# Fourier mixing and soft mixture of experts on one core: mirror rows folded in place, weights placed in freed tiles, one text order for all queues

## The chip, the cores and the metric

The kernel runs on one core of one Trainium2 chip. The metric is device time in microseconds of one execution, inputs and output in HBM. Engines are named as in the profile: PE is TensorE, DVE is VectorE, ACT is ScalarE, POOL is GpSimd, SP is the sync engine, whose queue issues all DMAs here.

## The reference

All tensors are float32. The first part is the real part of a two-dimensional Fourier transform of each of 8 sequences; the second routes all 19,968 tokens softly through 32 slots of 8 experts.

```python
X = np.fft.fft(x, axis=1)                     # x: 8 x 2496 x 256
x = np.fft.fft(X, axis=2).real.reshape(19968, 256)
logits = x @ phi                              # phi: 256 x 32
d = softmax over the tokens of logits         # per slot
slot_input = (d.T @ x).reshape(8, 4, 256)
for e in range(8):
    h = np.maximum(slot_input[e] @ w1[e], 0)  # w1: 8 x 256 x 1024
    slot_out[e] = h @ w2[e]                   # w2: 8 x 1024 x 256
c = softmax over the slots of logits          # per token
return c @ slot_out
```

## The kernel before

The 8 sequences are worked on as 4 pairs (`NPAIR`). The transform is never written out: logits come from x and a transformed phi, and the slot inputs come from x weighted by back-transformed softmax weights. As the output of a real transform has mirrored parts, each row of x is first added to its mirror row (the fold). A pair has four x tiles (t = 0 to 3) of 128 x 2560: plain rows in the first half of the columns, mirror rows in the second.

The parts, each a function named by its letter, for pair p:

- `load_x` (L174): one DMA of 1,280 KB per tile into one of 5 "ring" buffers. All 16 are issued in order.
- a (L230): the fold into a new tile eo (12 buffers), on DVE for the first tile and on POOL for the other 15 (L233); DVE transposes it into xT (L235; 4 buffers).
- z (L237): PE multiplies xT by the transformed phi (wz) into four PSUM banks; z of half h needs two xT tiles.
- t (L252): four DVE transposes bring the banks into zt (L257), after a memset on POOL (L254).
- b (L259): PE does the first transform stage (tile `a`, L266), ACT evicts.
- c (L269): for each half `hf`, PE does the second stage (lp, lm; L278, L279); ACT and DVE form the logits lt (L280 to L283); DVE takes maxima mx (L286); PE transposes them (mt, L288); DVE reduces and spreads them (L290, L292); PE transposes back (L293); DVE copies the result nm (L295); ACT takes exp into d (L298); POOL forms sum and difference dpm (L300, L301).
- e, d (L304, L322): PE transforms dpm back; ACT evicts to esb and dsb.
- u (L340): PE multiplies the weights by the folded rows eo (L354) into a bank, and ACT keeps the sum of the pair.

Then m (L389) joins the four pairs to slot inputs, l (L433) and v (L447) are the two layers of the experts in two halves, r (L459) gives rh. For the token softmax, s (L473) transposes lt, x, y, g (L490 to L508) do maximum, exp and division, q (L510) transposes the result to ct, and o (L518) multiplies ct by rh, evicts alternately by ACT and DVE into ring buffers and writes the output, 20 tiles.

The weights (w1 8.4 MB, w2 8.4 MB) are loaded by `load_w` (L373) in 22 DMAs after all x loads: five ring buffers, twelve eo buffers, four xT buffers and one more ring buffer take them (`WTILES`, L128), so each waits until the tile that it replaces has been used.

Order: `ORDER` (L29) lists the parts with their pair and half. `in_order` (L550) chains the instructions of each named engine in this order; up to r that is PE alone (`CHAIN = ("PE",)`), from r on PE, DVE, ACT and POOL. DVE, ACT, POOL and SP are ordered by the scheduler's own estimate before that. In `ORDER`, c of a half holds everything from lp to dpm, so that on PE the maxima's two transposes of half 0 come before lp of half 1.

Of the kernel before, what the change touches and what calls it, by code (L numbers as in the profile page):

```python
# [134 lines left out]
def _build(nc, tc, xh, phih, w1h, w2h, cins, where, out):  # L135
# [4 lines left out]
    with ctx:  # L140
# [197 lines left out]
        anchor = {}  # L338

        def part_u(p):  # L340
            ps = bank3(f"tok{p}")
            for h in range(2):
                for g in range(4):
                    pe.matmul(
                        ps[32 * g : 32 * g + 32, 0:1], dsb[p][:, 0, h, 0, 0, :], C("onehot"),
                        start=h == 0, stop=h == 1, tile_position=(0, 32 * g),
                    )
            sc.copy(tok[:, p : p + 1], ps[:, 0:1])
            ub = pu.tile([128, 512], F32, name=f"u{p}", tag="u")
            rows = [(h, ah, q) for h in range(2) for ah in range(2) for q in range(NQ)]  # L350
            for cc in range(10):
# [10 lines left out]
            ubs.append(ub)
            if p == NPAIR - 1:
                anchor["u"] = last.ins

        for p in range(NPAIR):
            for t in range(4):
                if (p, t) not in xt:
                    load_x(p, t)
# [3 lines left out]
        def load_w():  # L373
            cs.append(cp.tile(list(cins[4].shape), F32, name="cs4"))
            nc.sync.dma_start(cs[4], cins[4])
            for k, (first, kind, n) in enumerate(WTILES):
                t = {"ring": ring, "eo": eu, "et": et}[kind](f"w{k}")
                src, of, bw = (w1h, w1t, 512) if first else (w2h, w2t, D)
# [260 lines left out]
```

## Time and profile before

| | |
|---|---|
| median of 3 runs | 251.22 us (249.47, 252.27, 251.22) |
| the profiled execution | 249.02 us, its span 247.2 us |
| busy: PE, DVE, ACT, POOL | 68%, 44%, 31%, 32% |
| DMA | 59.83 MB, mean 242 GB/s over the span |
| chain that ended last, by engine | PE 41%, DVE 26%, DMA 14%, issue 5%, ACT 4%, POOL 4% |
| mean granted clock of PE | 0.861 |

The span runs from the first to the last instruction of the execution. The chain is the work that ended last, followed back from the end: at each step to what released it. "Issue" is time in which an engine waited for nothing that the profile shows. PE does each float32 matmul as two recorded instructions, so xcounts on PE are twice the number of matmuls in the program (transposes are single).

### The profile page before, as it was taken

To read this page: it belongs to the slowest core of one execution; us is meant where nothing else is said; L and a number is where in the kernel's file an instruction comes from. 1 tells how busy PE (TensorE), PEld (TensorE's weight loads), DVE (VectorE), ACT (ScalarE), POOL (GpSimd) and SP (SyncE) were. 2 spreads that over 40 slices of the span, in tenths; PEclk is the share of its full clock that TensorE was granted. 3 is DMA by queue.
4 is the path that set the end of the run, shared out by engine and by line. 5 is a ranking of instruction groups with operands and counts; after the bars stand their busy time and mean duration, and the time that the engine had idled before them with its cause. 6 is when DMAs were issued, how large, how long until landed. Compare 5 with 4: busy or idle time off the path is not lost.

```text
span 247.2 us, 5345 instructions
## 1 busy us (share of the span) xinstructions
PE 168.4 (68%) x2320; PEld 106.7 (43%) x2320; DVE 108.4 (44%) x183; ACT 75.7 (31%) x176; POOL 78.5 (32%) x55
## 2 busy tenths in 40 slices
PE   0576309559755986648879549959994989878800
PEld 0465208258522564514566125644462354344500
DVE  0543271444844046441004440040776689996410
ACT  2000003322324222332025331401541578653400
POOL 0288699841003892032000032000354144440000
PEclk9999999659985799965999957997999799997555
DMA  6999999994000099200846007592200399999995
GB/s 217 424 425 420 425 426 434 427 431 193 3 0 0 3 347 422 90 0 33 295 186 215 0 3 223 204 320 107 86 3 0 127 414 429 423 423 422 424 429 227
DMA packets 9672, 59.83 MB, mean 242 GB/s; under 512 B 1200, under 2 KB 1584, under 8 KB 5040
## 3 DMA queue, kind: packets, MB, share of 16 engines
q1 hardware_dynamic: 9648, 59.48, 60.0%
q8 instruction: 18, 0.29, 0.5%
q14 instruction: 6, 0.05, 0.1%
HBM read 39.03 MB, written 20.45 MB: 241 GB/s over the span
## 4 chain that ended last, share of the span: by engine, by line
PE 41%; DVE 26%; DMA 14%; issue 5%; ACT 4%; POOL 4%; SPq 1%; DVEq 0%; ACTq 0%
DMA x<-xh 10%; PE u L354 10%; PE z L245 7%; DVE o L536 5%; PE a L266 5%; DMA out<-o 4%; DVE zt L257 4%; PE e L313 4%; PE h L438 3%; DVE mx L286 3%; PE po L531 2%; POOL eo L233 2%; ACT d L298 2%; DVE cm L505 2%; PE lp L278 2%
## 5 line engine op out<-in xcount | busy, mean ns | idle before, releaser
L233 POOL TENSOR_TENSOR eo<-x 128x1280 f32<-128x1280 f32 x15 | 43.3, 2894 | 15.4 <-DMA x<-xh 15.0
L531 PE MATMUL po<-ct,rh 32*128 32x512 f32 (+2 forms) x192 | 35.2, 630 | 5.3 <-DVE o L536 1.9
L235 DVE STREAM_TRANSPOSE xT<-eo 128x1280 f32<-128x1280 f32 x16 | 23.9, 1502 | 32.5 <-PE z L245 18.4
L245 PE MATMUL z<-xT,wz 32*64 32x160 f32 x1024 | 27.5, 358 | 7.3 <-issue 3.8
L245 PEld LDWEIGHTS z<-xT,wz 32*64 32x64 f32 x1024 | 23.3, 161 | 10.9 <-issue 5.9
L536 DVE COPY o<-po 128x512 f32<-128x512 f32 (+1 forms) x40 | 24.6, 661 | 7.2 <-DMA out<-o 5.0
L536 ACT COPY o<-po 128x512 f32<-128x512 f32 (+1 forms) x40 | 21.0, 579 | 18.7 <-DMA out<-o 9.8
L531 PEld LDWEIGHTS po<-ct,rh 32*128 32x128 f32 x192 | 18.0, 209 | 17.5 <-DVE o L536 7.9
L300 POOL TENSOR_TENSOR dpm<-d 120x384 f32<-120x384 f32 (+1 forms) x8 | 7.4, 928 | 55.8 <-ACT d L298 45.4
L354 PE MATMUL u<-eo,ds 128*32 128x256 f32 x320 | 24.5, 476 | 0.0
L495 POOL TENSOR_TENSOR c<-c,cm 128x512 f32<-128x512 f32 (+1 forms) x8 | 10.0, 1264 | 42.2 <-DVE cm L494 41.2
L298 ACT ACTIVATE d<-lt,nm 120x128 f32<-120x128 f32 x44 | 13.7, 389 | 29.9 <-DVE nm L295 29.9
L266 PE MATMUL a<-cs,zt 128*120 128x128 f32 x88 | 13.0, 315 | 13.2 <-DVE zt L257 13.2
L266 PEld LDWEIGHTS a<-cs,zt 128*120 128x120 f32 x88 | 12.1, 217 | 15.4 <-DVE zt L257 15.4
L257 DVE STREAM_TRANSPOSE zt<-z 128x320 f32<-128x320 f32 x16 | 10.6, 788 | 17.4 <-PE z L245 17.4
L354 PEld LDWEIGHTS u<-eo,ds 128*32 128x32 f32 x320 | 13.3, 138 | 9.5 <-issue 7.0
L267 ACT COPY o<-a 120x512 f32<-120x512 f32 (+1 forms) x12 | 6.6, 549 | 33.1 <-PE a L266 32.9
L282 DVE TENSOR_TENSOR lt<-lt,lm 120x384 f32<-120x384 f32 (+1 forms) x8 | 4.2, 521 | 25.1 <-PE lm L279 18.1
L288 PE MATMUL mt<-cs,mx 120*6 120x120 f32 (+1 forms) x8 | 2.6, 327 | 18.2 <-DVE mx L286 18.2
L508 POOL TENSOR_TENSOR c<-c,cm 128x512 f32<-128x512 f32 (+1 forms) x8 | 10.1, 1263 | 10.0 <-DVE cm L507 6.4
L335 ACT COPY ds<-d 128x320 f32<-128x320 f32 x16 | 6.8, 425 | 15.5 <-PE d L329 14.3
L313 PE MATMUL e<-cs,dpm 120*64 120x120 f32 x176 | 10.6, 269 | 1.1 <-issue 1.1
(91 smaller groups left out, 189.2 us busy)
## 6 DMA issues: line engine op xcount, KB each, us to landing
x<-xh SPq DMA_DIRECT2D x16, 1280.0 KB, 12.3
out<-o SPq DMA_DIRECT2D x15, 1024.0 KB, 8.4
w<-w2h SPq DMA_DIRECT2D x12, 640.0 KB, 5.8
w<-w1h SPq DMA_DIRECT2D x5, 1280.0 KB, 7.3
out<-o SPq DMA_DIRECT2D x4, 896.0 KB, 9.7
w<-w1h SPq DMA_DIRECT2D x3, 512.0 KB, 4.7
out<-o SPq DMA_DIRECT2D x4, 256.0 KB, 4.5
cs<-c SPq DMA_DIRECT2D x1, 528.0 KB, 16.0
```

Source lines behind the costliest of these rows:

```text
L233: (v if (p, t) == (0, 0) else gp).tensor_tensor(e, x[:, :XW], x[:, XW:], op=ALU.add)
L235: v.transpose(xT[p, t], e)
L245: pe.matmul(zb[p][i][64 * ah : 64 * ah + 64, 160 * h : 160 * h + 160], wz[r, j % 4, j // 4, :], xv[r, :, j, :], start=j == 0, stop=j == 7, ...
L257: v.transpose(o[:, i], zb[p][i][:, :320].rearrange("p (x s) -> p x s", s=32))
L266: pe.matmul(ps[:120, i * 128 : i * 128 + 128], w, C("wa"), start=True, stop=True)
L298: sc.activation(d[:, g], L[:, g], AF.Exp, bias=nm[:, g : g + 1], scale=1.0)
L313: pe.matmul(ps[64 * k : 64 * k + 64, 120 * i : 120 * i + 120], dpm[p, hf][:, k, 3 * j + i, :], C(name), start=True, stop=True, tile_positi ...
L354: last = pe.matmul(ub[32 * g : 32 * g + 32, 0:D], dsb[p][:, k, h, ah, q, :], eo[p, 2 * h + ah][:, D * q : D * q + D], start=cc == 0, stop= ...
L495: gp.tensor_tensor(c, c, m[:, 0].unsqueeze(2).to_broadcast([128, n, NSLOT]), op=ALU.subtract)
L508: gp.tensor_tensor(c, c, m[:, 1].unsqueeze(2).to_broadcast([128, n, NSLOT]), op=ALU.mult)
L531: pe.matmul(po[:, j * w : j * w + w], rh[0][rows, 128 * dc : 128 * dc + 128], t[rows, r0 * NSLOT : r0 * NSLOT + w], start=True, stop=True, ...
L536: (v.tensor_copy if n_ev[0] % 2 else sc.copy)(ot[:, o : o + w * len(dcs)], po[:, : w * len(dcs)])
```

## The change

- x: each tile is loaded by two DMAs of 640 KB, plain rows into half of a ring buffer (8 buffers now, so that all 16 plain tiles stay on chip), mirror rows into one of 5 `xm` buffers. The fold is now part f and adds the mirror rows into the plain tile in place; eo is that view. Pair 0's four folds are on DVE, the other twelve on POOL.
- Weights: 19 tiles at seven steps k in the order, each in the home that has come free by then: ring, `xm`, xT, `sa` and `d` buffers. One array holds w1 and w2.
- Parts: z is cut into four pieces; c is cut into c (matmuls and ACT's eviction), n (lt, and both halves' maxima in one go after half 1), i (maxima transposed, reduced, spread), j (transposed back, exp) and p (dpm). dpm is formed on DVE, but for the difference of pair 3, on POOL. The memset of zt goes to DVE. u is cut in two. Token softmax for pairs 0 and 1 stands partly before m and l. A pair's ct is one tile.
- Order: `in_order` now chains PE, DVE, ACT, POOL and SP from the first part to the last, in a new `ORDER`, in which work of neighbouring pairs is interleaved.

```diff
-RING, NEO, NET = 5, 12, 4
+RING, NXM, NET = 8, 5, 4
-HT = ["se", "et"]
-LD = "0 1 00 p 01 02 2 03 10 11 3 12 13".split()
-CHAIN = ("PE",)
+HT = ["se", "se", "xm", "xm"]
+LD = "00 0 1 p 01 02 2 03 10 11 3 12 13".split()
 ORDER = (
-    "a00 a01 w00 z00 a02 a03 z01 t00 b00 c00 a10 c01 a11 z10 e00 a12 e01 a13 z11 t10 d00 b10 c10 a20 c11 a21 u00 z20 "
...
+    "t00 b00 a10 c00 c01 n00 n01 i00 a11 i01 j00 a12 j01 p00 a13 p01 "
+    "z10 z11 z12 z13 e00 t10 e01 b10 a20 a21 c10 d00 c11 a22 a23 n10 n11 "
+    "z20 z21 i10 z22 i11 j10 z23 j11 t20 u00 p10 u01 k00 k10 p11 b20 a30 a31 a32 a33 e10 e11 c20 c21 n20 n21 d10 "
...
 WTILES = (
-    [(1, "ring", 5)] * 5 + [(1, "eo", 2)] * 3 + [(1, "eo", 1)]
-    + [(0, "et", 5)] * 4 + [(0, "eo", 5)] * 8 + [(0, "ring", 4)]
+    [(0, "ring", 5, 0)] * 2 + [(1, "xm", 2, 0)] * 5 + [(2, "et", 2, 1)] * 4
+    + [(3, "ring", 4, 2), (3, "ring", 0, 10), (4, "sa", 0, 5)]
+    + [(5, "ring", 0, 10)] * 2 + [(6, "d", 0, 3)] * 2 + [(7, "ring", 0, 10), (7, "ring", 0, 7)]
 )
...
+        def load_x(p, t):
+            ah, h = t % 2, t // 2
+            if h == 0:
+                xt[p, ah] = ring(f"x{p}_{ah}")
+            eo[p, t] = xt[p, ah][:, XW * h : XW * h + XW]
+            xm[p, t] = xmir(f"xm{p}_{t}")
+            nc.sync.dma_start(eo[p, t], xh[p, t, :, :XW])
+            nc.sync.dma_start(xm[p, t], xh[p, t, :, XW:])
...
+        def part_f(p, t):
+            if (p, t) not in eo:
+                load_x(p, t)
+            (v if p == 0 else gp).tensor_tensor(eo[p, t], eo[p, t], xm[p, t], op=ALU.add)
 
         def part_a(p, t):
-            x = xt[p, t]
-            eo[p, t] = e = eu(f"eo{p}_{t}")
-            (v if (p, t) == (0, 0) else gp).tensor_tensor(e, x[:, :XW], x[:, XW:], op=ALU.add)
             xT[p, t] = et(f"xT{p}_{t}")
-            v.transpose(xT[p, t], e)
+            v.transpose(xT[p, t], eo[p, t])
...
-            gp.memset(zt[p][:, 40 * NSLOT :], 0.0)
+            v.memset(zt[p][:, 40 * NSLOT :], 0.0)
...
+        def part_p(p, hf):
+            n = GH[hf][1]
+            d = ds_[p, hf]
             q = tagged([120, 2, 6, NA], f"dpm{p}_{hf}", "dpm", 2)
-            gp.tensor_tensor(q[:, 0, :n], d[:, :n, 0], d[:, :n, 1], op=ALU.add)
-            gp.tensor_tensor(q[:, 1, :n], d[:, :n, 0], d[:, :n, 1], op=ALU.subtract)
+            v.tensor_tensor(q[:, 0, :n], d[:, :n, 0], d[:, :n, 1], op=ALU.add)
+            (gp if p == 3 else v).tensor_tensor(q[:, 1, :n], d[:, :n, 0], d[:, :n, 1], op=ALU.subtract)
             dpm[p, hf] = q
...
-                if ins.engine not in [ENG[x] for x in names]:
+                if ins.engine not in ENG.values():
```

The first place is DVE's queue around the zt transposes of pair 0; xT1_2 is the transposed x tile 2 of pair 1, eo1_2 its fold on POOL, z0_0 a PSUM bank of pair 0. Before:

```order
L235 STREAM_TRANSPOSE xT1_0_340<-eo1_0_338 128x1280
L235 STREAM_TRANSPOSE xT1_1_370<-eo1_1_368 128x1280
L235 STREAM_TRANSPOSE xT1_2_459<-eo1_2_457 128x1280
L257 STREAM_TRANSPOSE zt0_286<-z0_0_146 128x10x32
L257 STREAM_TRANSPOSE zt0_286<-z0_1_147 128x10x32
L257 STREAM_TRANSPOSE zt0_286<-z0_2_148 128x10x32
L257 STREAM_TRANSPOSE zt0_286<-z0_3_149 128x10x32
```

And now, on DVE at the same place (x0_1 holds the folded tile 3 of pair 0 in one half, lt0 the logits of pair 0):

```order
L247 STREAM_TRANSPOSE xT0_3_212<-x0_1_79 128x1280
L267 MEMSET zt0_318 128x40
L270 STREAM_TRANSPOSE zt0_318<-z0_0_140 128x10x32
L270 STREAM_TRANSPOSE zt0_318<-z0_1_141 128x10x32
L270 STREAM_TRANSPOSE zt0_318<-z0_2_142 128x10x32
L270 STREAM_TRANSPOSE zt0_318<-z0_3_143 128x10x32
L247 STREAM_TRANSPOSE xT1_0_342<-x1_0_90 128x1280
L304 TENSOR_TENSOR lt0_344<-lt0_344,lm0_0_346 120x6x64
```

The transposes of pair 1 have moved behind the zt transposes of pair 0.

The second place is DVE's queue behind the maxima of pair 0, half 1 (mex0_1 the spread maximum, nm0_0 and nm0_1 the negated maxima for exp). Before:

```order
L292 TENSOR_SCALAR mex0_1_354<-mall_94 5x120
L295 COPY nm0_1_357<-mt0_1_351 120x5
L235 STREAM_TRANSPOSE xT2_0_622<-eo2_0_620 128x1280
L235 STREAM_TRANSPOSE xT2_1_652<-eo2_1_650 128x1280
L235 STREAM_TRANSPOSE xT2_2_793<-eo2_2_791 128x1280
```

And now, on DVE (d0_0 is the exp of half 0, dpm0_0 its sum and difference):

```order
L320 TENSOR_SCALAR mex0_1_373<-mall_106 5x120
L328 COPY nm0_0_376<-mt0_0_363 120x6
L247 STREAM_TRANSPOSE xT1_2_385<-x1_0_90 128x1280
L328 COPY nm0_1_388<-mt0_1_370 120x5
L340 TENSOR_TENSOR dpm0_0_396<-d0_0_378 120x384
L341 TENSOR_TENSOR dpm0_0_396<-d0_0_378 120x384
L247 STREAM_TRANSPOSE xT1_3_399<-x1_1_94 128x1280
L340 TENSOR_TENSOR dpm0_1_401<-d0_1_390 120x320
L341 TENSOR_TENSOR dpm0_1_401<-d0_1_390 120x320
```

The dpm operations have come to DVE's queue, between pair 1's last two transposes and behind the last.

The third place is PE's queue in c of pair 1 (lp1_0 and lm1_0 are banks of half 0, mt1_0 the transposed maxima, tok0 the first bank of u of pair 0). Before:

```order
L278 MATMUL lp1_0_593<-o11_574,cs2_69 120x384
L279 MATMUL lm1_0_594<-o11_574,cs2_69 120x384
L288 MATMUL mt1_0_602<-cs0_67,mx1_0_600 6x120
L293 MATMUL mt1_0_602<-cs0_67,mex1_0_605 120x6
L278 MATMUL lp1_1_624<-o11_574,cs2_69 120x320
L279 MATMUL lm1_1_625<-o11_574,cs2_69 120x320
L288 MATMUL mt1_1_633<-cs0_67,mx1_1_631 5x120
L293 MATMUL mt1_1_633<-cs0_67,mex1_1_636 120x5
L344 MATMUL tok0_654<-cs3_70,ds0_549 32x1 x8
```

And now, on PE (d0_00 is a bank of d of pair 0, z2_0 one of z of pair 2):

```order
L293 MATMUL lp1_0_596<-o11_573,cs2_69 120x384
L294 MATMUL lm1_0_597<-o11_573,cs2_69 120x384
L369 MATMUL d0_00_602<-e0_536,cs2_69 32x320 x4
L369 MATMUL d0_01_608<-e0_536,cs2_69 32x320 x4
L369 MATMUL d0_10_614<-e0_536,cs2_69 32x320 x4
L369 MATMUL d0_11_620<-e0_536,cs2_69 32x320 x4
L293 MATMUL lp1_1_626<-o11_573,cs2_69 120x320
L294 MATMUL lm1_1_627<-o11_573,cs2_69 120x320
L258 MATMUL z2_0_643<-xT2_0_591,wz_105 64x160
```

The maxima's transposes have left this place (they stand between pieces of z of pair 2), and d of pair 0 has come between the halves.

## Rows read from the trace of the kernel before

**Rows 1.** Page, section 5: group | busy us, mean ns | idle before, releaser.

```profile
L233 POOL TENSOR_TENSOR eo<-x 128x1280 f32<-128x1280 f32 x15 | 43.3, 2894 | 15.4 <-DMA x<-xh 15.0
...
L235 DVE STREAM_TRANSPOSE xT<-eo 128x1280 f32<-128x1280 f32 x16 | 23.9, 1502 | 32.5 <-PE z L245 18.4
...
L288 PE MATMUL mt<-cs,mx 120*6 120x120 f32 (+1 forms) x8 | 2.6, 327 | 18.2 <-DVE mx L286 18.2
```

**Rows 2.** Timeline of the start, 0 to 60 us: start us, us, instruction, idle before.

```profile
7.81 1.49 DVE L233 TENSOR_TENSOR eo<-x 128x1280 f32<-128x1280 f32 x1 [7.81 <-DMA x<-xh]
...
17.82 2.89 POOL L233 TENSOR_TENSOR eo<-x 128x1280 f32<-128x1280 f32 x1 [0.81 <-DMA x<-xh]
...
22.31 4.54 PE L245 MATMUL z<-xT,wz 32*64 32x160 f32 x120 [2.18 <-DVE xT L235]
```

**Rows 3.** Chain that ended last, pair 0: start us, us, what.

```profile
34.29 2.63 DVE zt L257 x4
36.97 5.05 PE a L266 x22
...
49.49 0.50 DVE lt L282
...
50.53 0.83 DVE mx L286
...
52.69 3.87 PE z L245 x128
```

**Rows 4.** The same chain, pairs 1 and 2.

```profile
79.63 6.07 PE u L354 x80
85.70 2.38 PE z L245 x128
88.08 2.41 PE e L313 x44
...
98.99 2.66 PE a L266 x22
101.67 0.91 PE lp L278 x2
102.58 0.66 PE lm L279 x2
...
106.98 1.86 ACT d L298 x6
```

**Rows 5.** The same chain, from d of pair 3 to rh.

```profile
156.10 2.34 PE d L329 x30
158.56 4.41 PE u L354 x80
...
168.94 4.97 PE h L438 x32
173.91 1.28 PE cT L480 x11
175.19 3.64 PE h L438 x32
...
190.88 0.43 DVE rh L469
```

**Rows 6.** Windows: stretch us, busy us and count of PE, PEld, DVE, ACT, POOL; PEclk; DMA; GB/s.

```profile
15.00:21.00 6.00, 4.58 (x128) 4.07 (x128) 2.27 (x3) 0.00 (x0) 5.00 (x3) 1.00 1.00 417
...
79.00:83.00 4.00, 3.95 (x53) 2.10 (x57) 0.17 (x1) 1.61 (x6) 1.66 (x3) 0.50 0.01 4
...
154.00:163.00 9.00, 8.54 (x162) 6.58 (x157) 0.00 (x0) 3.45 (x9) 0.00 (x0) 1.00 0.65 228
```

**Rows 7.** Waits of the whole span (SP's are the queue's): waiter <- releaser: us, times, longest.

```profile
PE z L245 <- issue: 3.8, 3, 1.6
...
PE e L313 <- issue: 1.1, 1, 1.1
...
SPq L380 <- PE u L354: 51.5, 12, 20.4
```

More of the change, by code (lines that the diff above doesn't have):

```diff
@@ L337, in _build, with part_u @@
         ubs = []
[L338 to L351, printed above, removed]
+        def part_u(p, half):
+            if half == 0:
+                ps = bank3(f"tok{p}")
+                for h in range(2):
+                    for g in range(4):
+                        pe.matmul(
+                            ps[32 * g : 32 * g + 32, 0:1], dsb[p][:, 0, h, 0, 0, :], C("onehot"),
+                            start=h == 0, stop=h == 1, tile_position=(0, 32 * g),
+                        )
+                sc.copy(tok[:, p : p + 1], ps[:, 0:1])
+                ubs.append(pu.tile([128, 512], F32, name=f"u{p}", tag="u"))
+            ub = ubs[-1]
+            rows = [(h, ah, q) for ah in range(2) for h in range(2) for q in range(NQ)]
+            for cc in range(5 * half, 5 * half + 5):
                 for g in range(4):
                     k, (h, ah, q) = g // 2, rows[2 * cc + g % 2]
-                    last = pe.matmul(
+                    pe.matmul(
                         ub[32 * g : 32 * g + 32, 0:D],
@@ L359, in part_u, with load_w @@
                     )
-            if p < NPAIR - 1:
+            if half == 1 and p < NPAIR - 1:
                 sc.copy(usb[:, p, :], ub[:, :D])
[L362 to L369, printed above, removed]
-        w1t, w2t = [], []
[L373 to L378, printed above, removed]
-                o = len(of) * bw * 128
-                nc.sync.dma_start(t[:, : n * bw], src[o : o + 128 * n * bw].rearrange("(p c) -> p c", p=128))
-                of += [t[:, i * bw : i * bw + bw] for i in range(n)]
+        w1t, w2t = [], []
+        def load_w(step):
+            if step == 0:
+                cs.append(cp.tile(list(cins[4].shape), F32, name="cs4"))
+                nc.sync.dma_start(cs[4], cins[4])
+            o = 0
+            for k, (at, kind, n1, n2) in enumerate(WTILES):
+                w = 512 * n1 + 256 * n2
+                if at == step:
+                    if kind in ("ring", "xm", "et"):
+                        t = {"ring": ring, "xm": xmir, "et": et}[kind](f"w{k}")
+                    else:
+                        t = tagged([128, w], f"w{k}", kind, 2)
+                    nc.sync.dma_start(t[:, :w], wh[o : o + 128 * w].rearrange("(p c) -> p c", p=128))
+                    w1t.extend(t[:, 512 * i : 512 * i + 512] for i in range(n1))
+                    w2t.extend(t[:, 512 * n1 + D * i : 512 * n1 + D * i + D] for i in range(n2))
+                o += 128 * w
         sm = cp.tile([128, 40], F32, name="sm")
@@ L545, in _build, with in_order @@
         ENG = {
-            "PE": mybir.EngineType.PE, "DVE": mybir.EngineType.DVE,
+            "PE": mybir.EngineType.PE, "DVE": mybir.EngineType.DVE, "SP": mybir.EngineType.SP,
             "ACT": mybir.EngineType.Activation, "POOL": mybir.EngineType.Pool,
         }
-        def in_order(names, f, *a):
+        def in_order(f, *a):
             n = len(traced)
@@ L570, in _build @@
         }
-        names = CHAIN
         for what in ORDER:
-            if what[0] == "r":
-                names = tuple(ENG)
-            in_order(names, parts[what[0]], int(what[1]), int(what[2]))
+            in_order(parts[what[0]], int(what[1]), int(what[2]))
 def kernel(x, moe_phi, moe_w1, moe_w2):
@@ L591 @@
     phih = moe_phi.reshape(2, 128, NSLOT).transpose(1, 0, 2)
[L593 to L600 removed]
     w1b = moe_w1.reshape(2, 4, 2, 128, 2, 512).transpose(0, 4, 2, 1, 3, 5).reshape(W1N, 128, 512)
[L603 removed]
     w2b = moe_w2.reshape(2, 4, 32, 32, D).transpose(0, 2, 1, 3, 4).reshape(2, 8, 4, 128, D).reshape(W2N, 128, D)
+    i1 = i2 = 0
+    wh = []
+    for _, _, n1, n2 in WTILES:
+        wh.append(np.concatenate([w1b[i1 : i1 + n1].transpose(1, 0, 2).reshape(128, -1),
+                                  w2b[i2 : i2 + n2].transpose(1, 0, 2).reshape(128, -1)], axis=1).ravel())
+        i1, i2 = i1 + n1, i2 + n2
     tabs, where = _tables()
[L607 removed]
+    arrays = {"xh": xh, "phih": phih, "wh": np.concatenate(wh)}
     arrays.update({f"c{i}": t for i, t in enumerate(tabs)})
@@ L616 @@
     with tile.TileContext(nc, schedule_with_timeline_sim=True) as tc:
-        _build(nc, tc, *ins[:4], ins[4:], where, out)
+        _build(nc, tc, *ins[:3], ins[3:], where, out)
     r = _run(nc, [arrays], core_ids=[0])
```

79 lines of the change are left out of this document (45 added, 34 removed), and 6 rows, old and new, of the table ORDER.

## The prediction

> **What bounds the kernel now.** I read the chain of waits first, in order of time, because the page's busy shares average over stages: TensorE (PE) is busy 68% of the span, yet it is often idle just where the chain passes. Three stretches appear. (1) Up to 37 us the chain is pair 0's fold. The last x tile of pair 0 is on chip at 17.8 us, its fold on POOL takes 2.9, its transpose and the last z matmuls end near 26.9 [rows 2], but VectorE's (DVE's) four zt transposes run only at 34.3 and PE's `a` matmuls at 37.0 [rows 3]. DVE had pair 1's transposes queued ahead of them, and these waited for POOL. (2) From 37 to 163 us the pairs follow one another. The `a` matmuls of pairs 0 and 2 begin at 37.0 and 99.0 [rows 3, 4], 31 us a pair. Inside a pair PE waits for DVE twice in each half: from lt at 49.5 to the next z at 52.7 PE has only two small transposes of 0.33 us [rows 1, 3]. (3) From 163 us: 6 us for the slot inputs, two expert halves, then rh, ready at 190.88 + 0.43 = 191.3 [rows 5], and 55.9 us to the span's end at 247.2 in which the output is written.
>
> Then the clock. In pair 1's stretch 79 to 83 us the granted clock is 0.50, the 1.2 GHz level, and u takes 6.07 us; in 154:163, after PE had been busy without a gap, it is 1.00 and u takes 4.41 [rows 4 to 6]. The row 15:21 says 1.00, but there the z matmuls run at half speed: half a pair takes 4.54 us at 22.3 and 2.38 at 85.7 [rows 2, 4, 6]. So I go by durations early on.
>
> **The change, step by step.** The work on PE, ScalarE and in bytes stays the same; it is mostly order. I add up the path to rh from durations of rows.
>
> *Pair 0 up to `a`.* The folds of pair 0 go from POOL to DVE: 1.49 instead of 2.89 us [rows 1, 2]. Bytes ahead of x03 are the same, so it lands at 17.8 again. Fold 1.49, transpose 1.50, z 4.54, zt 2.63 [rows 1 to 3], a little for the moved memset and handovers: `a` starts at 28.3, 8.7 earlier than now.
>
> *Pair 0's logits and pair 1's z.* `a` 5.05 [rows 3]; c half 0 takes 0.91 + 0.66 = 1.57 [rows 4]; half 1 has 320/384 of the columns, 1.31 at full clock and 2.6 at half. I take 2.6, the clock having come up late here: 37.5. Now both halves' lt come before both maxima: two at 0.50, then 0.83 and 1.00 for the maxima [rows 3], the longer by 6/5, 40.3. Steps i and j cost what lies between the end of mx (50.53 + 0.83 = 51.36) and the next z at 52.69, 1.33 for one half [rows 3]; the second adds 0.6, and one transpose of pair 1 lies between, 1.5: 43.7, where z10 begins. Behind it DVE has nm, the transpose of x12, the new dpm ops, the transpose of x13. The dpm ops on DVE are a form that before does not show. Bounds: the lt ops at 0.50 (one operand in PSUM), and POOL's two-operand rate 2.89 x 384/1280 = 0.87; below 0.50 I see no reason. I take 0.55, DVE's fold rate being half POOL's. Exp 1.86 [rows 4] ends at 45.3, dpm 46.4, transpose 47.9, second z half 50.4, zt 53.0: pair 1's `a` at 53.1. The e matmuls hide beside zt.
>
> *Pairs 1 to 3 on a full PE.* Here d of the previous pair stands between the halves of c, and z of the next one between i and j, so what PE waited for runs beside other matmuls. A round is `a` 2.66, c 2.88, e 2.41, z 2 x 2.38 = 4.76, four small transposes 1.3, and d with tok and u 162.97 - 156.10 = 6.87 [rows 1, 4, 5]: 20.9 against 31. Pair 1's round lacks e (done), 18.5, plus 1.1 because z of pair 2 needs the PSUM bank that the last lt op frees: `a` of pair 2 at 72.7, of pair 3 at 93.6. Then `a`, e, c, d, u and three small transposes, 15.8: 109.4. The u at full clock alone is worth 1.66 in each of three rounds [rows 4, 5].
>
> *Pair 3's tail is not covered.* After its j: nm 0.2, exp 1.86, dpm on POOL 0.9, e half 1.3; the second exp stands behind two evictions of s (0.5 each, an estimate from the lt op, [rows 3]), takes 1.55, dpm 0.75, e 1.1, then d, tok, u 6.87: 124 with handovers. Token transposes s (1.28 a pair, [rows 5]) fill PE's gaps.
>
> *To rh.* m as now, 168.94 - 162.97 = 5.97; l 2 x 3.64; v has 128 matmuls of u's shape, 4.41 x 128/80 = 7.06; r two copies, two products and rh, 1.7 [rows 5]. Token softmax of pairs 0 and 1 has mostly run before l. Sum 146.0. PE also stands still without a cause that the profile names, 3.8 + 1.1 = 4.9 us in four places of z and e [rows 7]; nothing in the change removes it: 150.9. Some thirty more handovers between blocks at 0.05: 152.4.
>
> *Loads.* Of x nothing is saved: 12 folds on POOL from 20.9 need at least 35 us, and SP sends three plain tiles ahead of mirror x12, some 3 us later for it. Pair 1's last fold then ends near 36.5, needed at 46.4; pair 3's near 60, needed near 84. Cover 10 and 24 us; nothing is charged. Weights now wait 51.5 us on u [rows 7]. In the new order the first 5.8 MB go out after u of pair 0 (72.7) and at 417 GB/s [rows 6] are in at 87; the last 2.2 MB after pair 3's u (124), in at about 131; v needs them at 137. Cover 6 us; if it is gone, each us is a us.
>
> *After rh* the same 20 output tiles leave in the same order. Eight ring buffers instead of five end evictions' waits, but the output is a stream at the rate of the memory; I take 55.9 again, 54.5 if the merged ct, finished earlier, helps.
>
> Sum 152.4 + 55.9 = 208.3 of span; the profiled run took 249.02 with a span of 247.2, 1.8 around it: **210 us**. It stands 2.2 below the median of 251.22, within the spread of 249.47 to 252.27.
>
> **A rule that speaks against it.** The trace shows transposes of DVE (one input) beside POOL's folds with neither longer: means 1.50 and 2.89 [rows 1]. It shows no DVE instruction with two SBUF inputs beside a POOL fold. The Trainium skill, SBUF — State Buffer, section Who interferes with whom, says that such a pair contends: the second to start is held until the first ends. By it the four dpm ops of pair 0 would each wait for a fold; by the first sentence alone they would not.
>
> **Rivals.**
> - *DVE and POOL shut each other out in pair 0* (the rule above names it). The four dpm ops at 45 to 49 us meet POOL's folds, 2.89 each and back to back until 60. A mechanism of this place: the first waits half a fold on average, the next ones up to one; two lie ahead of the transpose of x13 and so of z: 1.4 + 2.9 = 4.3; the other two delay e and zt by up to 3 more. 214 to 217. For it: POOL has no gap there. Against: no row shows it. Chance 0.17.
> - *Supply is late*: weights or the unexplained stillstands of PE grow, since 16.8 MB of weights, 40 us at 417 GB/s [rows 6], now load beside full matmuls. The 4.9 grow by 7 (six more places at the 1.2 us they have now) and v is late by 5: 222. Against: the 6 us cover. Chance 0.12.
> - *The pipelining does not take hold and PE stays at 1.2 GHz.* Between 43.7 and 144 us PE has some 80 us of work in my sum. At half clock it doubles, 290 us, slower than before. It decides from about half of that stretch at 0.50, since 41 us are to be given back. For it: 79:83 at 0.50 though PE was 99% busy [rows 6]. Against: there PE came out of waits like those of [rows 3], and the full stretch got 1.00. Chance 0.03.
> - *Better*: the clock comes up in pair 0 (c and z 2.5 earlier), no stillstands (4.9), a quicker start of the output (1.4): 201. Chance 0.05.
> - The forecast: 0.63.
>
> **How the numbers follow.** Predicted 210. The low end is the better case, 200; the high end the late supply with a little over, 224. The forecast alone: 205 to 215. Faster by over 1% (what a measurement of this kernel can tell) is every case but the half clock and an unforeseen stall of SP or DVE: 0.95; within 1%: 0.01; slower: 0.04.
>
> **What would show it.** Right: zt of pair 0 at about 25.5 instead of 34.3; `a` matmuls of the four pairs near 28, 53, 73 and 94; a granted clock of 1.00 from 55 to 125; u at 4.4 in all pairs; rh near 152; output 56 us. Wrong: dpm ops on DVE that take or wait 2 us and more; PE waiting for w in v; gaps of PE before z of pairs 2 and 3; rh later than 165.

## The result, and the profile after

The changed kernel takes **208.36 us** (median of 4 runs: 206.57, 208.46, 208.25, 209.06), beside 250.34 us of the kernel before (4 runs, 248.34 to 252.27): a ratio of 0.833, with a 95% interval of 0.825 to 0.842. The profiled execution took 206.57, with a span of 204.8, 42.4 less than before. The ratios, here and below, leave out executions that ran in a slower state, the medians do not, so the two can differ by about 1%.

Page, the engines' busy shares and two of the 40-slice rows (slices of 5.1 us):

```profile
PE 153.8 (75%) x2320; PEld 105.3 (51%) x2320; DVE 123.5 (60%) x204; ACT 75.6 (37%) x176; POOL 58.4 (29%) x34
...
PE   0475849296998999989999699399989897785000
...
PEclk9999557955799999999999999979999999669655
```

PE's busy time fell from 68% of 247.2, or 168.4 us, to 153.8 us for the same matmuls: 14.6 us less, as they ran faster (u in 380 ns on the mean instead of 476). 5.4 us of this lie in the matmuls of the output (35.2 before, 29.8 now), where the time hardly changed; so faster matmuls are some 9 us of the gain before rh, and the rest is idle time that went. From the eleventh slice to the 22nd (51 to 113 us) PE is nearly full, and one slice in its clock is up. The 5s of the last row lie in pair 0 and at the start of pair 1, and behind PE's last matmul.

The start, timeline of 18 to 30 us (start us, us, instruction, idle before and what ended it):

```profile
18.20 1.49 DVE L243 TENSOR_TENSOR x<-x,xm 128x1280 f32<-128x1280 f32 x1 [0.72 <-DMA xm<-xh]
19.72 1.51 DVE L247 STREAM_TRANSPOSE xT<-x 128x1280 f32<-128x1280 f32 x1
...
21.29 4.54 PE L258 MATMUL z<-xT,wz 32*64 32x160 f32 x120 [3.25 <-DVE zt L267]
...
25.85 2.67 DVE L270 STREAM_TRANSPOSE zt<-z 128x320 f32<-128x320 f32 x4 [4.56 <-PE z L258]
...
28.57 1.85 PE L279 MATMUL a<-cs,zt 128*120 128x128 f32 x7 [2.74 <-DVE zt L270]
```

Against [rows 2, 3] the last fold takes 1.49 on DVE, zt follows the z matmuls at once, and `a` begins at 28.57 instead of 36.97.

The chain that ended last, pairs 1 and 2 and the passage to rh (start us, us, what):

```profile
64.36 0.50 DVE lt L305
...
64.99 2.41 PE z L258 x122
...
71.87 4.34 PE u L395 x80
76.22 2.59 PE a L279 x22
...
97.86 2.59 PE a L279 x22
...
123.22 4.42 PE u L395 x80
...
133.81 8.18 PE h L478 x64
142.00 6.96 PE so L493 x128
...
150.15 0.44 DVE rh L509
```

Where [rows 4] passed from PE to DVE, ACT and back, the chain of two rounds is now PE alone but for two lt operations in the first. A round lasts 20.3 us (55.9 to 76.2) and 21.6 (to 97.9); it was 31. The u blocks on the chain take 4.34 to 4.42; 6.07 stood in [rows 4]. rh ends at 150.6 and was at 191.3, so 40.7 of the 42.4 us came before rh; behind it are 54.2, which were 55.9.

But pair 0 holds something that the sum did not contain. DVE, timeline of 40 to 56 us:

```profile
43.19 0.56 DVE L340 TENSOR_TENSOR dpm<-d 120x384 f32<-120x384 f32 x1 [0.46 <-ACT d L331]
43.67 3.25 DVE L341 TENSOR_TENSOR dpm<-d 120x384 f32<-120x384 f32 x1
46.84 1.50 DVE L247 STREAM_TRANSPOSE xT<-x 128x1280 f32<-128x1280 f32 x1
48.27 1.74 DVE L340 TENSOR_TENSOR dpm<-d 120x320 f32<-120x320 f32 x1
49.94 3.17 DVE L341 TENSOR_TENSOR dpm<-d 120x320 f32<-120x320 f32 x1
...
53.08 2.64 DVE L270 STREAM_TRANSPOSE zt<-z 128x320 f32<-128x320 f32 x4
```

and POOL, timeline of 20 to 70 us:

```profile
31.85 29.82 POOL L243 TENSOR_TENSOR x<-x,xm 128x1280 f32<-128x1280 f32 x10 [3.77 <-DMA xm<-xh]
```

The four dpm operations take 8.7 us. They end at 43.75, 46.92, 50.01 and 53.11, that is 3.1 to 3.2 apart: one for each fold of POOL, however short it is. The transpose between them (one input) takes its usual 1.50. In pair 1, where POOL is silent, DVE's timeline has the same operations unheld:

```profile
74.29 0.55 DVE L340 TENSOR_TENSOR dpm<-d 120x384 f32<-120x384 f32 x1
74.76 0.53 DVE L341 TENSOR_TENSOR dpm<-d 120x384 f32<-120x384 f32 x1
75.22 0.48 DVE L340 TENSOR_TENSOR dpm<-d 120x320 f32<-120x320 f32 x1
75.62 0.48 DVE L341 TENSOR_TENSOR dpm<-d 120x320 f32<-120x320 f32 x1
```

So pair 0 pays 8.72 - 2.04 = 6.7 us of DVE time, of which 2.7 delay the transpose that the second z half needs. PE's timeline there:

```profile
48.39 4.54 PE L258 MATMUL z<-xT,wz 32*64 32x160 f32 x120 [1.88 <-DVE xT L247]
...
55.93 2.66 PE L279 MATMUL a<-cs,zt 128*120 128x128 f32 x22
```

Windows by stage (stretch; busy us and count of PE, PEld, DVE, ACT, POOL; PEclk; DMA share; GB/s), to be set beside [rows 6]:

```profile
45.00:54.00 9.00, 7.12 (x172) 6.13 (x158) 9.00 (x7) 0.00 (x0) 9.00 (x4) 0.50 1.02 418
54.00:73.00 19.00, 17.67 (x398) 12.53 (x398) 13.23 (x22) 8.13 (x21) 7.67 (x3) 0.99 0.13 52
73.00:93.00 20.00, 19.35 (x425) 13.65 (x417) 13.45 (x22) 8.56 (x23) 0.00 (x0) 1.00 0.82 314
...
134.00:137.00 3.00, 3.00 (x20) 0.64 (x16) 2.69 (x10) 0.08 (x1) 0.50 (x1) 0.64 0.00 0
```

Around the held operations the granted clock is at the 1.2 GHz level; the rounds have the 2.4 GHz level.

### The profile page after: what moved, and what is told of

It reads as the page before. It is cut to its first block, busy times and chain, and to the rows that moved or that the text cites. A ratio compares the mean times of both kernels' runs of the same rounds, so it can differ in the third digit from the quotient of the medians.

```text
span 204.8 us, 5356 instructions
## 1 busy us (share of the span) xinstructions
PE 153.8 (75%) x2320; PEld 105.3 (51%) x2320; DVE 123.5 (60%) x204; ACT 75.6 (37%) x176; POOL 58.4 (29%) x34
## 4 chain that ended last, share of the span: by engine, by line
PE 45%; DMA 19%; DVE 15%; issue 9%; ACT 1%; POOL 1%; SPq 1%; DVEq 0%; POOLq 0%
DMA x<-xh 11%; DMA xm<-xh 8%; PE z L258 8%; DVE o L579 7%; PE u L395 6%; PE po L574 5%; PE e L353 5%; PE h L478 4%; PE a L279 4%; PE so L493 3%; PE d L369 3%; DVE dpm L341 2%; PE lp L293 1%; DVE cm L545 1%; PE cT L520 1%
## 5 line engine op out<-in xcount | busy, mean ns | idle before, releaser
L243 POOL TENSOR_TENSOR x<-x,xm 128x1280 f32<-128x1280 f32 x12 | 35.6, 2997 | 25.6 <-DMA xm<-xh 25.6
L258 PE MATMUL z<-xT,wz 32*64 32x160 f32 x1024 | 30.7, 376 | 7.9 <-DVE zt L267 3.3
L574 PE MATMUL po<-ct,rh 32*128 32x512 f32 (+2 forms) x192 | 29.8, 617 | 4.5 <-DVE ct L554 2.1
L258 PEld LDWEIGHTS z<-xT,wz 32*64 32x64 f32 x1024 | 25.5, 170 | 11.9 <-DVE zt L267 3.5
L574 PEld LDWEIGHTS po<-ct,rh 32*128 32x128 f32 x192 | 16.7, 203 | 13.5 <-DVE o L579 7.8
L247 DVE STREAM_TRANSPOSE xT<-x 128x1280 f32<-128x1280 f32 x16 | 23.3, 1484 | 0.1
L395 PE MATMUL u<-x,ds 128*32 128x256 f32 x320 | 18.4, 380 | 0.0
L341 POOL TENSOR_TENSOR dpm<-d 120x384 f32<-120x384 f32 (+1 forms) x2 | 2.5, 1272 | 54.8 <-ACT d L331 54.8
L395 PEld LDWEIGHTS u<-x,ds 128*32 128x32 f32 x320 | 12.0, 110 | 4.2
L353 PEld LDWEIGHTS e<-cs,dpm 120*64 120x64 f32 x176 | 10.0, 144 | 2.9 <-DVE dpm L340 1.4
L243 DVE TENSOR_TENSOR x<-x,xm 128x1280 f32<-128x1280 f32 x4 | 6.0, 1492 | 8.8 <-DMA xm<-xh 8.7
```

The source lines that it names most:

```text
L243: (v if p == 0 else gp).tensor_tensor(eo[p, t], eo[p, t], xm[p, t], op=ALU.add)
L247: v.transpose(xT[p, t], eo[p, t])
L258: pe.matmul(zb[p][i][64 * ah : 64 * ah + 64, 160 * h : 160 * h + 160], wz[r, j % 4, j // 4, :], xv[r, :, j, :], start=j == 0, stop=j == 7, ...
L353: pe.matmul(ps[64 * k : 64 * k + 64, 120 * i : 120 * i + 120], dpm[p, hf][:, k, 3 * j + i, :], C(name), start=True, stop=True, tile_positi ...
L395: pe.matmul(ub[32 * g : 32 * g + 32, 0:D], dsb[p][:, k, h, ah, q, :], eo[p, 2 * h + ah][:, D * q : D * q + D], start=cc == 0, stop=cc == 9 ...
L574: pe.matmul(po[:, j * w : j * w + w], rh[0][rows, 128 * dc : 128 * dc + 128], t[rows, r0 * NSLOT : r0 * NSLOT + w], start=True, stop=True, ...
```

## The experiments

Three groups, each on one chip beside runs of the kernel before. The last column is the time from `a` of pair 0 to `a` of pair 1 in the profiled execution, the stretch in which pair 0's dpm lies; in the first profile of the changed kernel it is 27.4. All times in us.

| run | group | median (lowest to highest, runs) | ratio to before, 95% | span | a, pair 0 | a0 to a1 |
|---|---|---|---|---|---|---|
| a_ref | 1 | 206.71 (204.48 to 208.02, 4) | 0.814 to 0.827 | 202.7 | 26.31 | 26.6 |
| e1_pool_dpm0 | 1 | 204.34 (201.07 to 207.85, 4) | 0.797 to 0.811 | 204.4 | 28.37 | 25.3 |
| e2_gate | 1 | 202.96 (202.70 to 204.71, 4) | 0.805 to 0.815 | 201.2 | 27.83 | 24.6 |
| e3_ij_block | 1 | 217.62 (214.44 to 219.55, 4) | 0.850 to 0.870 | 212.7 | 25.83 | 27.0 |
| e4_pe_only | 2 | 234.70 (233.95 to 235.97, 4) | 0.941 to 0.952 | 231.9 | 44.60 | 31.4 |
| e5_late_weights | 2 | 207.73 (205.42 to 209.77, 4) | 0.827 to 0.841 | 205.5 | 28.18 | 28.3 |
| e6_before_split | 2 | 248.87 (one run) | | 247.1 | | |
| e7_pool0_dve3 | 2 | 204.55 (203.28 to 205.85, 6) | 0.819 to 0.830 | 201.5 | 27.98 | 24.6 |
| a_ref2 | 3 | 205.80 (204.61 to 207.80, 6) | 0.814 to 0.825 | 203.4 | 27.16 | 28.7 |
| e8_weights_held | 3 | 219.70 (219.36 to 224.07, 4) | 0.869 to 0.881 | 217.6 | 26.67 | 26.8 |
| e9_gate_dve3 | 3 | 203.31 (202.43 to 205.79, 6) | 0.805 to 0.814 | 202.3 | 26.41 | 25.6 |
| e10_pool_folds0 | 3 | 208.09 (205.63 to 209.05, 4) | 0.815 to 0.831 | 205.5 | 29.44 | 29.1 |

**The changed kernel again** (a_ref and a_ref2, no edit), as the yardstick of groups 1 and 3.

> The changed kernel itself, on the chip of the runs beside it, as their base. Span 204.8 us as before, ratio to the kernel before 0.833; the DVE dpm operations of pair 0 again near 0.56, 3.25, 1.74 and 3.17 us.

> The changed kernel once more, as the base of the three beside it: median 206 to 208.5, ratio 0.82 to 0.833.

206.71 and 205.80, with spans of 202.7 and 203.4. The dpm operations are held in both. What moves between executions is the start: the second z half of pair 0 took 2.43 in a_ref, 3.35 in a_ref2 and 4.54 in the first profile, and `a` came at 26.3, 27.2 and 28.6.

**Is it the folds that hold dpm?** Two ways to part them. e1 forms pair 0's dpm on POOL, between its folds:

```diff
-... f10 f11 f12 f13 f20 f21 f22 f23 f30 f31 f32 f33 "
+... f10 f11 f12 f13 f20 f21 "
...
-    "t00 b00 ... a13 p01 "
+    "t00 b00 ... a13 p01 f22 f23 f30 f31 f32 f33 "
...
-            v.tensor_tensor(q[:, 0, :n], ..., op=ALU.add)
-            (gp if p == 3 else v).tensor_tensor(q[:, 1, :n], ..., op=ALU.subtract)
+            (gp if p == 0 else v).tensor_tensor(q[:, 0, :n], ..., op=ALU.add)
+            (gp if p in (0, 3) else v).tensor_tensor(q[:, 1, :n], ..., op=ALU.subtract)
```

> Pair 0's dpm goes to POOL's own queue, between its fold of x21 and that of x22. Theory (DVE and POOL hold each other off): no two-input operation of DVE meets a fold; the transpose of x13 no longer stands behind a held operation and ends near 44.2 instead of 48.3; z of pair 1 runs without a gap, a of pair 1 starts at 51.5 to 54 instead of 55.9; span 2 to 4.5 us shorter. Rival (dpm on DVE is slow in pair 0 for a reason of its own, such as ScalarE writing d beside it): POOL's dpm is slow too, over 1.3 us each, and the span gains under 1 us.

e2 leaves dpm on DVE and makes POOL pause instead: the same move of f22 to f33 in the order, and a tiny sum on POOL that reads dpm, ahead of them.

```diff
+            if p == 0 and hf == 1:
+                gate = tagged([120, 2], "gate", "gate", 1)
+                gp.tensor_tensor(gate, q[:, 0, 0, :2], q[:, 1, 0, :2], op=ALU.add)
```

> dpm of pair 0 stays on DVE, but POOL pauses after its fold of x21 until that dpm is done (a tiny sum of two of its columns stands in POOL's queue). Theory (held off by the folds): with POOL silent the four DVE operations take 0.5 to 0.6 us each, 2.1 in all instead of 8.7, a of pair 1 starts 2 to 5 us earlier, and the folds end some 3 us later, which nothing feels; span 2 to 4.5 us shorter. Rival (slow for a reason of its own): they still take 2 to 3 us, and the span stays within 1 us.

DVE of e2, timeline of 38 to 54 us:

```profile
41.75 1.76 DVE L340 TENSOR_TENSOR dpm<-d 120x384 f32<-120x384 f32 x1 [0.46 <-ACT d L331]
43.43 0.55 DVE L341 TENSOR_TENSOR dpm<-d 120x384 f32<-120x384 f32 x1
43.90 1.50 DVE L247 STREAM_TRANSPOSE xT<-x 128x1280 f32<-128x1280 f32 x1
45.33 0.44 DVE L340 TENSOR_TENSOR dpm<-d 120x320 f32<-120x320 f32 x1
45.70 0.47 DVE L341 TENSOR_TENSOR dpm<-d 120x320 f32<-120x320 f32 x1
```

and POOL of e2, timeline of 28 to 70 us:

```profile
31.64 11.45 POOL L243 TENSOR_TENSOR x<-x,xm 128x1280 f32<-128x1280 f32 x4 [3.79 <-DMA xm<-xh]
46.25 0.19 POOL L345 TENSOR_TENSOR gate<-dpm 120x2 f32<-120x2 f32 x1 [3.16 <-DVE zt L267]
```

The last fold before the pause ends at 31.64 + 11.45 = 43.09. The first dpm, begun inside it, ends 0.42 later, at 43.51; the other three, with POOL silent, take 0.44 to 0.55. Same engine, same operation, same data, only POOL's fold taken away: that shows the cause. In e1 POOL's four take 1.00, 1.00, 0.86 and 0.85, and nothing is held either.

The gain in time is less sharp. By the medians e2 is 3.75 us under a_ref and e1 2.4 (by the ratios 2.6 and 4.2). In the profiled executions the second z half of pair 1 takes 2.44 in e2, 3.39 in a_ref and 4.54 in the first profile. `a` of pair 1 begins at 52.4 in e2, 53.7 in e1 and 52.9 in a_ref, so the 2 to 5 us that were expected of e2 do not show against a_ref, whose pair 0 came 1.5 us earlier. Counted from `a` of pair 0 they part: the seven profiled executions with folds beside all of pair 0's dpm (the first one, a_ref, a_ref2, e3, e5, e8, e10; e4 has another order) take 26.6 to 29.1, the four in which they are gone or partly gone (e1, e2, e7, e9) 24.6 to 25.6.

**Pair 3 as well.** e7 is e1 with pair 3's difference on DVE too, e9 is e2 with the same:

```diff
-            (gp if p == 3 else v).tensor_tensor(q[:, 1, :n], ..., op=ALU.subtract)
+            v.tensor_tensor(q[:, 1, :n], ..., op=ALU.subtract)
```

> dpm of pair 0 on POOL between two folds, and dpm of pair 3, where POOL has no folds left, wholly on DVE. Theory: as with dpm of pair 0 on POOL alone, a of pair 1 2 to 4 us earlier than in the changed kernel; in pair 3 the second operation takes 0.55 on DVE instead of 1.37 on POOL, e of pair 3 0.3 to 0.5 us earlier a half; ratio to the kernel before 0.80 to 0.81, some 3 us under the changed kernel. Rival (the earlier part is given back later): within 1 us of the changed kernel.

> POOL pauses for pair 0's dpm as before, and dpm of pair 3 is wholly on DVE. Theory: 2.5 to 3.5 us from the pause, 0.4 to 0.8 from pair 3: median 203 to 204.5, 3 to 4 us under the changed kernel beside it. Rival (given back later, in the experts or the output): within 1 us of it.

In the changed kernel pair 3's sum on DVE and difference on POOL start together, and POOL's are the longer for it. POOL of the changed kernel, timeline of 100 to 126 us:

```profile
115.47 1.37 POOL L341 TENSOR_TENSOR dpm<-d 120x384 f32<-120x384 f32 x1 [53.80 <-ACT d L331]
117.84 1.18 POOL L341 TENSOR_TENSOR dpm<-d 120x320 f32<-120x320 f32 x1 [1.00 <-ACT d L331]
```

1.37 and 1.18, where POOL alone took 1.00 and 0.86 in e1. With both on DVE the second group of e matmuls starts 2.97 us after exp (109.17 to 112.14 in e7) instead of 3.36 (113.53 to 116.89): 0.4 us. That is too little to be seen in a median: e7 is 3.2 under e5, which runs as the changed kernel does (below), and e9 2.5 under a_ref2 (3 to 4 were expected), in the range that e1 and e2 had without it. The four versions that free pair 0's dpm in whole or in part gain 2.4 to 3.75 by the medians, all of one sign, though only e1's interval is clear of its copy's; those of e2, e7 and e9 overlap with theirs at the edge. e2 and e9, at 203 us, are below both kernels: 0.81 of the kernel before, where the copies beside them, a_ref and a_ref2, have 0.82. In e9 the second operation still met POOL's last fold before the pause and took 3.25.

**How much is the order of the other engines?** e4 chains only PE before r, with everything else of the change left in:

```diff
+        names = [("PE",)]
...
-                if ins.engine not in ENG.values():
+                if ins.engine not in [ENG[x] for x in names[0]]:
...
+            if what[0] == "r":
+                names[0] = tuple(ENG)
```

> The changed kernel with TensorE alone chained to the text order up to r, as in the kernel before; the other queues go by the scheduler's estimate. Theory (the text order on all queues carries the start): SP sends all nine plain tiles that are left ahead of mirror x12, 9 x 1.54 = 14 us, so POOL folds x12 at about 41 instead of 31.9, and zt of pair 0 stands behind the transpose of x12: a of pair 0 at 45 to 47 instead of 28, span 16 to 19 us longer, near 222. Rival (TensorE's order alone carries the gain): within 3 us of the changed kernel.

234.70. POOL, timeline of 10 to 80 us, and the operations on DVE, 30 to 80 us:

```profile
37.58 2.88 POOL L243 TENSOR_TENSOR x<-x,xm 128x1280 f32<-128x1280 f32 x1 [9.67 <-DMA x<-xh]
45.12 26.83 POOL L243 TENSOR_TENSOR x<-x,xm 128x1280 f32<-128x1280 f32 x9 [4.67 <-DMA xm<-xh]
```

```profile
40.48 1.51 DVE L247 STREAM_TRANSPOSE xT<-x 128x1280 f32<-128x1280 f32 x1 [11.04 <-POOL x L243]
41.92 2.62 DVE L270 STREAM_TRANSPOSE zt<-z 128x320 f32<-128x320 f32 x4
...
57.06 2.77 DVE L340 TENSOR_TENSOR dpm<-d 120x384 f32<-120x384 f32 x1 [1.18 <-ACT d L331]
59.75 3.25 DVE L341 TENSOR_TENSOR dpm<-d 120x384 f32<-120x384 f32 x1
62.93 3.18 DVE L340 TENSOR_TENSOR dpm<-d 120x320 f32<-120x320 f32 x1
66.03 3.17 DVE L341 TENSOR_TENSOR dpm<-d 120x320 f32<-120x320 f32 x1
```

The old fault of the start is back: a transpose of pair 1 waits on DVE for a fold, zt of pair 0 stands behind it (41.9), `a` comes at 44.6. The start costs the 16 us foreseen. Some 10 more, which were not foreseen, come behind it: all four dpm are held here (12.4 us) with pair 1's transposes after them, which makes `a` to `a` 3.1 longer than in e5, and the later rounds and the tail lose the rest. POOL's fold here begins at 37.58 and in e5 at 32.56, because SP sends the loads in another order: some 5 of the 16 us are SP's order (an estimate from these two starts), the rest DVE's; no run parts them. Against e5 on the same chip the order of the engines other than PE is worth 27.0 us by the medians; PE's order, the loads and the homes of the weights with the old way of ordering the rest are worth 251.41 - 234.70 = 16.7. By the ratios it is 28 and 13.

**And the pieces set between each other on PE?** e3 keeps all chains but puts steps i and j of pairs 1 and 2 back behind the maxima, ahead of d and of the next z:

```diff
-    ... c10 d00 c11 a22 a23 n10 n11 z20 z21 i10 z22 i11 j10 z23 j11 ...
+    ... c10 c11 n10 n11 i10 i11 j10 j11 d00 a22 a23 z20 z21 z22 z23 ...
```

(and the same with d10 and z30 to z33 for pair 2).

> On all engines i and j of pairs 1 and 2 stand right behind n, ahead of d of the pair before and of z of the next. Theory (what TensorE waited for now runs beside other matmuls): the waits come back, some 4.5 us of idle TensorE in each of two pairs, and with them a lower granted clock for part of d and z: span 8 to 13 us longer, 213 to 218. Rival (the gain comes from homes and loads, the place of i and j hardly matters): within 2 us of the changed kernel.

217.62, 10.9 over a_ref, in the range given. Windows of e3, the two rounds:

```profile
54.00:73.00 19.00, 15.22 (x334) 9.12 (x336) 9.46 (x18) 7.25 (x20) 7.51 (x3) 0.82 0.11 44
73.00:93.00 20.00, 16.85 (x190) 10.09 (x182) 14.46 (x25) 8.66 (x25) 0.00 (x0) 0.86 0.67 264
```

PE is idle for 3.8 and 3.2 us of these, and the clock falls with it; the rounds last 24.8 and 26.8 us (`a` at 52.8, 77.6 and 104.4).

**Pair 0's folds on POOL** (e10): all but the first, as before the change.

```diff
-            (v if p == 0 else gp).tensor_tensor(eo[p, t], eo[p, t], xm[p, t], op=ALU.add)
+            (v if (p, t) == (0, 0) else gp).tensor_tensor(eo[p, t], eo[p, t], xm[p, t], op=ALU.add)
```

> The folds of x01 to x03 of pair 0 go back to POOL. Theory (they stand on the path, 2.89 instead of 1.49 us, the last one alone counts): a of pair 0 starts 1.4 us later and the span is 1 to 2 us longer. Rival (what moved the start is only the place of zt): a within 0.5 us of the changed kernel's.

The last transpose of pair 0 starts at 20.59 instead of 19.53 in a_ref2, so the fold itself moved it by 1.06. `a` came 2.3 later, but 1.2 of this is the z half at 4.54 instead of 3.35, which differs between executions anyway. The medians are 2.3 apart with overlapping intervals: beyond the 1.06 of the trace no time is shown for this part.

**The weights.** e5 was to delay all weights but the first two tiles until pair 3's u, by moving their steps in the order:

```diff
-    ... u00 p10 u01 k00 k10 p11 ... k20 ... k30 ... k40 ... k50 ... k60 ... u31 k70 "
+    ... u00 p10 u01 k00 p11 ... u31 k10 k20 k30 k40 k50 k60 k70 "
```

> All weights but the first ten blocks of w1 are issued after u of pair 3 instead of at six places before. Theory (the homes that come free early keep the weights off the path): 14.2 MB at 420 GB/s are 34 us, the last lands near 161 instead of some 133, v ends near 162 instead of 148, span 12 to 16 us longer. Rival (the weights have time enough behind u): within 2 us.

207.73: the expected 12 to 16 us did not appear, and the expectation was wrong about the edit, not about the chip. SP's rows say so, timeline of 65 to 150 us, a_ref2 first and e5 second:

```profile
73.90 52.87 SPq L418 DMA_DIRECT2D w<-wh  x20
74.21 53.07 SPq L418 DMA_DIRECT2D w<-wh  x20
```

The 20 weight transfers (20 tiles at eight steps, k00 to k70; the 19 at seven steps above are a miscount) begin and end as before. SP has no other transfer between these steps, so it waits for each home in turn, wherever the step stands in the text. The position of a step sets nothing here; the homes do. So e5 says nothing on the cover, and serves as a third copy of the changed kernel, on the chip of group 2.

e8 does what e5 was meant to do: the same move, and SP first issues a small copy of `tok`, which is complete only when pair 3's tok is, ahead of the weights.

```diff
+            if step == 1:
+                nc.sync.dma_start(cp.tile([128, NPAIR], F32, name="gate"), tok)
```

> As with the weights moved behind u of pair 3, but now SP's queue really is held there: ahead of the weights of step 1 SP issues a small copy of tok, which is complete only with the last pair. Theory (the homes that come free early keep the weights off the path): 14.2 MB at 420 GB/s from 125 on, the last lands near 161, v ends near 162 instead of 148; span 12 to 16 us longer. Rival (the weights have time enough behind u): within 2 us.

219.70, 13.9 over a_ref2, inside the range given. PE now waits for weights in v (waiter, releaser: us, times, longest; in the first layer it is 1.3 us):

```profile
PE so L495 <- DMA w<-wh: 6.7, 5, 2.0
```

and the chain of e8:

```profile
120.68 3.25 DMA gate<-tok
...
137.72 19.36 DMA w<-wh
...
157.13 3.81 PE so L495 x34
```

The weights are now the chain and end at 157.1; the last 34 of v's matmuls start at 157.13, and in a_ref2 at about 143.9 (140.77 + 6.96 - 3.81): 13.2 later. Up to there e8 was ahead of a_ref2 (`a` of pair 3 at 93.6 and 96.3), so from the same start it would be nearer 16. In the changed kernel no such wait is among PE's waits: its last weights are issued at 127.7, DMA moves nothing in 134:137, and v begins at 142.0. The cover is there, some 8 us of it, and with it gone the loss shows.

**PE standing still without a cause.** e6 is the kernel before with its weight transfers cut into pieces of 512 columns, to see whether large transfers on the queues are what holds PE.

```diff
-                nc.sync.dma_start(t[:, : n * bw], src[...])
+                for c0 in range(0, n * bw, 512):
+                    c1 = min(c0 + 512, n * bw)
+                    nc.sync.dma_start(t[:, c0:c1], full[:, c0:c1])
```

> The kernel before, each weight transfer cut into pieces of 512 columns (2 KB for each partition instead of up to 10 KB). Theory (TensorE's unexplained stillstands of 1.1 to 1.6 us are its own instructions waiting behind long weight packets): they shrink to 0.6 us or less, 4.9 us in sum falls to under 2, span 2 to 4 us shorter. Rival (packet length has no part in it): 1.1 to 1.6 us each, 4 to 6 in sum, span within 1 us of 247.2.

The span is the same (247.1, where 247.2 was), and z's wait of this kind 2.2 us in 3 places instead of [rows 7]'s 3.8 and 1.1. It proves nothing, as the changed kernel shows: there the sum was 1.1, 0.4, 0.4 and 0 in four executions of it (e5 among them), and e1, with almost the same program, had 2.0 before z and 1.9 before e.

The traces themselves say more than this edit. Count the records of PE, of PEld and of PE's sequencer in order of start: every stop of 0.15 us or more that no releaser explains, 26 in 14 traces, before and after the change, comes a multiple of 256 records after the 194th or 195th. Each ends 1.2 to 1.6 us after a transfer of 16 KB on the instruction queue has ended (queue 8 of the page; 18 such transfers in an execution of some 4,660 records, about 256 records each). So what the theory said of PE's own instructions agrees with every stop: PE stood until the next ones had come. What it said of weight packets does not: in the kernel before, the transfers that ended the four stops took 0.88 to 0.97 us, no longer than others. No edit has tested this, and why such a transfer comes too late in one execution and not in another stays open. In e2 and e7 one such stop of 1.9 us, in e of pair 0, even held `a` of pair 1 (zt had ended at 50.6 in e2, `a` began at 52.4), so these versions may have some more to give.

## Why the prediction was right, and which terms were not

Predicted 210 (200 to 224), measured 208.36: the range, the forecast's own range of 205 to 215 and the direction hold, and the forecast's mechanism is the one that ran. Of its signs of being wrong one came, dpm operations on DVE of 2 us and more; PE waits for no weights in v, its gaps before z of pairs 2 and 3 are 0.8 us and less, and rh comes at 150.6. The span was to be 208.3 and is 204.8. The terms differ more than their sum:

- *Pair 0 up to `a`*: 28.3 predicted, 28.57 measured. Its steps are all in the rows (1.49, 1.51, 4.54, 2.67). That 4.54 was the half-speed price of [rows 2]; a_ref shows that it can also be 2.43.
- *Pair 0's logits and pair 1's z*: `a` of pair 1 at 53.1 predicted, 55.93 measured, 2.5 us lost. **The step that failed is "I take 0.55" for the dpm operations on DVE.** It is right for DVE without POOL (0.44 to 0.55) and wrong beside back-to-back folds (up to 3.25). e2 and e7, with little or none of that overlap, run the stretch in 24.6 us; the forecast had 53.1 - 28.3 = 24.8. So the first rival's mechanism was at work inside the likeliest case. Its price, 4.3 on z and up to 3 more, was near in DVE time (6.7 in all) and too high for the transpose (2.7), and only 2.4 to 3.75 came out of the medians when it was taken away: the third and fourth dpm ran beside the second z half, which ended at 52.93 and they at 53.11. The rule that was weighed there (the Trainium skill, SBUF — State Buffer, section Who interferes with whom: a DVE instruction with two SBUF inputs and a GpSimd one that reads SBUF exclude each other) agrees with this trace, 3.25 beside folds against 0.53 without. A chance of 0.17 for this rival was too low.
- *Rounds on a full PE*: 19.6 and 20.9 predicted, 20.3 and 21.6 measured. 0.5 and 0.6 of this are stops without a cause, which stood in a term of their own. The wait for the last lt was put at 1.1 and is 0.8.
- *Pair 3's tail*: from `a` to the end of u 30.4 predicted (93.6 to 124), 29.8 measured.
- *To rh*: m 6.17 against 5.97, v 6.96 against 7.06, r 1.63 against 1.7, but the first layer 8.18 against 7.28. Here the sum took the second half's 3.64 of [rows 5] twice, though the first half stands there with 4.97. It runs partly at a low clock (0.64 in 134:137), after m in which PE waits 2.9 us for DVE. With the 3.6 us by which u of pair 3 is late this gives 150.6.
- *Stops without a cause and thirty handovers*: 4.9 + 1.5 added, 1.1 measured and already within the rounds. **These two terms were mis-sized**, and this is what paid for the held dpm and the first layer: without them the sum to rh is 146.0, 4.6 below the measured 150.6. That the total came out so near is in this part luck. I had argued that nothing in the change removes the stops; the copies show that they are no fixed property of the kernel: one program has them in one execution and not in the next.
- *After rh*: 55.9 predicted, 54.2 measured, the 54.5 of the other case. 54.0 in both copies. Whether the merged ct or the eight buffers did it was not tried.
- *Cover of the weights*: 6 us predicted, some 8 measured, and the price "each us is a us". e8 bears it out: the last v of e8 stands 13.2 later than in a_ref2, and so does the end, by 14.2 of span.
- *The clock rival (290 us)* fell: 54 to 125 us has 0.99 to 1.00. e3 shows what it hangs on here: the same matmuls, with 3 to 4 us of waiting back in each round, get 0.82 to 0.86.

By the runs of group 2 the gain, 43.7 us there, is 27.0 for the order of the engines other than PE, given all the rest (e4), and 16.7 for all the rest without it (28 and 13 by the ratios). What the homes of the weights, the eight buffers and PE's own order bring each by itself within the latter was not tried. Undoing the interleaving of i and j alone, on all engines, costs 10.9 (e3); this overlaps with both and is no third part.

## What to carry to other kernels

When several engines work on neighbouring tiles, give every engine's queue an order, not only that of the bottleneck: the same PE program with the other engines left to a scheduler was 27 us slower, 16 of them at the start, where a transpose that waited for a fold stood in front of ready ones and the loads came in another order. Before moving an elementwise operation with two SBUF inputs to DVE, look at what POOL does at that moment; an operation of 0.55 us next to folds costs up to a whole fold each time, and letting POOL pause for 3 us paid some 2.5 to 3.75 us. To delay a transfer in an experiment, give its queue something to wait for; a later place in the text does nothing where the queue waits on buffers anyway.

## What the runs showed of the hardware that was not expected

- DVE's two-input operations and POOL's folds take turns, and DVE gets one turn for each fold: in e2 an operation begun inside a fold ended 0.42 us after that fold, and so did one in e9. In e4 four in a row took 2.77, 3.25, 3.18 and 3.17. The folds pay little for it: 2,997 ns on the mean of twelve against 2,894 [rows 1], or 1.2 us in all.
- The first part of an execution is not repeatable to 2 us: the same 120 z matmuls of pair 0 took 4.54, 3.35 or 2.43 us in three executions of one kernel.
- The held operations cost PE twice, by the wait and by the speed of what follows, but the second price differs between executions. In 45:54 the changed kernel was granted 0.50 after a wait of 1.9 us for the transpose, and a_ref 0.81 after 2.0; the second z half took 4.54 and 3.39. e2, with a wait of 0.5, had 1.00 and 2.44, but so had e8, held like the others: 1.00 and 2.40 after a wait of 2.2. So the second price is not tied to the wait alone.
- PE's stops that no releaser explains come at fixed places in its stream of instructions, 256 records or a multiple of it apart, and end 1.2 to 1.6 us after 16 KB of instructions have come in (26 stops in 14 traces, 0.2 to 1.9 us each).
